# Windowed attention with a gated two-weight product on one core: a 1e-9 moved to ScalarE, three weight conversions moved to VectorE, slots re-ordered

## The chip, the cores and the metric

One NeuronCore of one Trainium2 chip runs the whole program. The metric is the time of one execution in device microseconds (us). Three timed runs of the kernel before gave 752.46 us as their median (751.79 to 753.01); the profiled execution took 752.39 us.

## The reference

```python
scores = q @ k.T / sqrt(64)                      # 4 batches, 8 heads, 768 positions
keep = (pos_k < n_sink) | (0 <= pos_q - pos_k < window)        # 4 sinks, window 128
a = exp(where(keep, scores, -1e9) - rowmax)
a = a / (sum(a) + 1e-9)
x = (a @ v)                                      # to 3072 tokens x 512
out = ((x @ w_a) * (x @ w_b)) @ w_out            # 512 -> 1536 -> 512, float32
```

The weights come as 64-bit words and are turned into float32 on the chip.

## The kernel before

**Tiles and chunks.** Tokens go in tiles of 128. The first tile of each batch is handled by `first_tiles` (L514). The other 20 tiles form six chunks (`CHUNKS`, L229): two of two tiles, four of four tiles. The gated product ("MoE") of a chunk runs while the attention of the next one is computed: stage c=0 (`moe`) works on the first tiles, c=1 and c=2 (`moe2`) on the two small chunks, c=3 to 6 (`moe7`) on the large ones; c=6 has no attention beside it. In the trace c=1 lies at about 145 to 224 us, c=2 to 294, c=3 to 407, c=4 to 525, c=5 to 643.

**Number form.** A float32 operand is split into a high part, rounded to TensorE's fp32r, and a low part, the rest. One product is three matmuls: high by high, high by low, low by high. ScalarE makes high parts by a copy, VectorE or GpSimd (POOL) low parts by a subtraction.

**Slots.** `run` (L1372) and the MoE functions emit the instructions; `keep_order` (L1169) then fixes each engine's order to the order of emission, so an engine never passes over a waiting instruction. A slot is one group of matmuls with what `slot` (L1283) emits behind it: `finish` (the end of the attention scores of the step before: 1e-9 added at L724, reciprocal L725, two scalings by ScalarE L727, a copy L728), the slot's own read of PSUM, `between` (as many attention steps as `PACE` wants), `step_late` (work that was put off, one stage a slot), and `next_piece` (three output matmuls at L1204 for an earlier block of MoE). In `moe2` a round j has three slots: the `a` product read by ScalarE (L990), the `b` product multiplied in by VectorE (L998), and the output products (L983); its g is split at L995 (ScalarE) and L996 (POOL; VectorE in the last round). In `moe7` a half-round has four: X (12 matmuls, read at L1248), Y (12, added at L1252), X again (12, L1258 to L1261), and a short one of 6 into Y (read at L1265). X and Y each have one PSUM bank, and from c=3 on the scores have one bank as well: a score product waits until VectorE has read the one before (L712, L713).

**Seven products.** `moe7` uses seven products in place of eight (the Winograd scheme). The weights' sums for it are made by `convert` (L1011) during c=1 and c=2: fetch two weights from DRAM (L1031), four sums on POOL (L1036, L1037, L1040, L1041), two high parts on ScalarE (L1051), two low parts on VectorE (L1055), each part sent to DRAM by SyncE's queue (L1048). `CONVERTS` says at which slot one begins: c=1 has seven (slots 0, 3, 8, 11, 16, 19, 24), c=2 five. The next chunk's own sums are made by `make_ops` (L1120) in six stages: differences on VectorE (L1141), high parts on ScalarE (L1134), low parts on VectorE (L1138). They begin in c=2 at slot `OPS_AT`, and in c=3 to 5 behind the first product of the last half-round. For c=2 the operand is split by `split_part` (L887, L890 and L891) at slots 34 to 36 of c=1.

**Attention.** Per head, POOL splits keys and queries (L418, L421), TensorE makes scores of a tile (L702), VectorE overwrites part of them and takes the row's limit (L712, L713), ScalarE the exponential with its sum (L715).

## Time and profile before

| | |
|---|---|
| median of three runs | 752.46 us |
| profiled execution | 752.39 us, its span 750.5 us |
| granted TensorE clock | 0.999 of full speed |
| busy: TensorE, its weight loads | 726.9 us (97%), 641.4 us (85%) |
| busy: VectorE, ScalarE, POOL | 475.9 us (63%), 385.0 us (51%), 354.2 us (47%) |

TensorE's row counts a matmul as busy until its modelled end, so idle TensorE time shows as waits, listed by what was waited for. A busy time of another engine includes what an instruction waits for after it was started.

### The profile page before, as it was taken

Reading aid. Unit: us, or ns where it says so; the run is one execution under the profiler, and the core shown is the slowest. Engines: PE = TensorE matmul, PEld = TensorE weight load, DVE = VectorE, ACT = ScalarE, POOL = GpSimd, SP = SyncE. Lnnn points to the kernel's source line nnn. Section 1 sums busy time; section 2 is a strip of 40 time slices with the busy share of each in tenths; the row PEclk is TensorE's granted clock in tenths of the full one; section 3 lists DMA queues with packets and bytes.
Section 4 is the critical chain, followed back from the end, with each engine's and each line's share of the span. In section 5 each row is a group of like instructions: output and inputs, shape, how many; then the busy total and the mean of one; then the engine's idle time right before and its main releaser. Section 6 shows DMA issues by size and latency. Waiting matters only on the chain.

```text
span 750.5 us, 14604 instructions
## 1 busy us (share of the span) xinstructions
PE 726.9 (97%) x4952; PEld 641.4 (85%) x4952; DVE 475.9 (63%) x1309; ACT 385.0 (51%) x1111; POOL 354.2 (47%) x378
## 2 busy tenths in 40 slices
PE   8999999999879999999999999999999999999997
PEld 6877777888769888898888988899899898899995
DVE  6899998365466757756648567755676654744322
ACT  6678775466456665545534554543365552444211
POOL 2200000144966793866733877743776723343430
PEclk9999999999999999999999999999999999999999
DMA  8999962388626587867785596876587666589641
GB/s 329 346 389 336 364 228 92 126 261 264 218 76 203 144 279 239 273 224 242 233 266 197 182 310 233 248 239 220 167 286 241 227 213 209 195 295 338 224 156 60
DMA packets 80642, 175.86 MB, mean 234 GB/s; under 512 B 8624, under 2 KB 26032, under 8 KB 80560
## 3 DMA queue, kind: packets, MB, share of 16 engines
q1 hardware_dynamic: 76960, 168.56, 67.1%
q10 hardware_dynamic: 3600, 6.30, 2.2%
q8 instruction: 41, 0.67, 0.4%
q14 instruction: 41, 0.34, 0.1%
HBM read 144.93 MB, written 29.88 MB: 233 GB/s over the span
## 4 chain that ended last, share of the span: by engine, by line
PE 78%; DMA 6%; POOL 6%; DVE 5%; ACT 3%; issue 1%; SPq 0%; ACTq 0%; POOLq 0%; DVEq 0%
PE o L1204 17%; PE a L906 7%; PE b L906 6%; PE o L933 5%; PE s L702 4%; PE av L745 4%; PE o L983 2%; PE t L733 2%; PE X_0b L1157 2%; PE X_2b L1157 2%; PE X_1b L1157 2%; PE X_2a L1157 2%; PE X_3a L1157 2%; PE X_5a L1157 2%; PE X_4a L1157 2%; PE X_4b L1157 2%
## 5 line engine op out<-in xcount | busy, mean ns | idle before, releaser
L715 ACT ACTIVATE p<-p,st 128x132 f32<-128x132 f32 x128 | 51.7, 404 | 87.7 <-DVE st L713 87.6
L1204 PE MATMUL o<-r_O,gh 128*128 128x512 f32 x288 | 93.8, 407 | 0.0
L1321 POOL TENSOR_TENSOR gl<-bu,gh 128x512 fp32r<-128x512 f32 x46 | 60.4, 1313 | 59.3 <-ACT gh L1318 58.4
L727 ACT ACTIVATE p<-p,st 128x132 f32<-128x132 f32 x128 | 45.0, 399 | 38.3 <-DVE st L725 38.1
L1036 POOL TENSOR_TENSOR s_a<-s_a 128x256 f32<-128x256 f32 x4 | 2.9, 736 | 123.3 <-PE o L933 113.6
L724 DVE TENSOR_SCALAR st<-st 128x2 f32<-128x2 f32 x64 | 33.1, 517 | 42.8 <-ACT p L715 42.8
L712 DVE COPY_PREDICATED s<-own,s 128x128 f32<-128x128 uint16 x128 | 36.9, 288 | 36.8 <-PE s L702 36.5
L1204 PE MATMUL o<-r_O,gl 128*128 128x512 f32 x144 | 56.5, 392 | 0.0
L1253 POOL TENSOR_TENSOR bu<-x 128x256 f32<-128x256 f32 x24 | 18.6, 775 | 72.4 <-DVE x L1252 72.4
L421 POOL TENSOR_TENSOR ks<-kr,ks 64x656 fp32r<-64x656 f32 x32 | 51.3, 1604 | 2.7
L1204 PEld LDWEIGHTS o<-r_O,gh 128*128 128x128 f32 x288 | 44.9, 189 | 2.6 <-issue 2.1
L702 PE MATMUL s<-ks,qh 128*128 128x260 f32 x128 | 39.0, 305 | 3.5 <-DVE st L713 1.9
L421 POOL TENSOR_TENSOR ql<-qr,qh 128x512 fp32r<-128x512 f32 x32 | 41.4, 1292 | 1.3
L906 PE MATMUL a<-x,w_a 128*128 128x256 f32 x288 | 40.2, 287 | 1.5 <-ACT x L890 1.5
L418 POOL TENSOR_SCALAR ks<-kr 64x656 fp32r<-64x656 f32 x32 | 24.5, 764 | 36.5 <-PE s L702 33.6
L735 DVE TENSOR_TENSOR pt<-t,tri 128x1024 f32<-128x1024 f32 x32 | 39.0, 1220 | 4.1 <-PE t L733 4.1
L713 DVE CUSTOM_DVE_ANT_0 p<-s,mg 128x132 f32<-128x132 f32 x128 | 37.8, 295 | 4.4
L906 PE MATMUL b<-x,w_b 128*128 128x256 f32 x288 | 39.3, 285 | 0.0
L906 PEld LDWEIGHTS a<-x,w_a 128*128 128x128 f32 x288 | 36.5, 188 | 2.7 <-ACT x L890 1.7
L1318 ACT CAST gh<-bu 128x512 fp32r<-128x512 f32 x48 | 29.2, 612 | 18.2 <-PE o L1204 11.9
L906 PEld LDWEIGHTS b<-x,w_b 128*128 128x128 f32 x288 | 36.2, 189 | 0.3 <-issue 0.2
L702 PE MATMUL s<-ks,ql 128*128 128x260 f32 x128 | 36.1, 282 | 0.0
(480 smaller groups left out, 2239.4 us busy)
## 6 DMA issues: line engine op xcount, KB each, us to landing
r_O<-d_O SPq DMA_DIRECT2D x36, 512.0 KB, 4.3
r_H_a<-d_H_a SPq DMA_DIRECT2D x24, 512.0 KB, 5.5
r_L_a<-d_L_a SPq DMA_DIRECT2D x24, 512.0 KB, 6.3
r_H_b<-d_H_b SPq DMA_DIRECT2D x24, 512.0 KB, 5.5
r_L_b<-d_L_b SPq DMA_DIRECT2D x24, 512.0 KB, 6.3
qr<-in_qT_dram SPq DMA_DIRECT2D x32, 256.0 KB, 3.8
raw_a<-in_wa_dram SPq DMA_DIRECT2D x12, 512.0 KB, 6.8
raw_b<-in_wb_dram SPq DMA_DIRECT2D x12, 512.0 KB, 6.5
```

The lines of the kernel that those rows point to most:

```text
L421: return self.nc.gpsimd.tensor_tensor(o, i, high.bitcast(F32), op=ALU.subtract)
L702: mm = nc.tensor.matmul(ps, lhsT=q[:, i * P:(i + 1) * P], rhs=ks[:, c0s[i]:c0s[i] + SW], start=n == 0, stop=n == 1)
L712: nc.vector.copy_predicated(ps[:, :P], self.own.bitcast(mybir.dt.uint16), ps[:, W:])
L713: nc.vector.tensor_tensor_reduce(out=p, in0=ps[:, :W], in1=self.mg[:, :W], scale=-0.125, scalar=BIG, op0=ALU.add, op1=ALU.min, accum_out=s ...
L715: nc.scalar.activation(p, p, AF.Exp, bias=st[:, 0:1], scale=-1.0, accum_out=st[:, 1:2])
L727: nc.scalar.mul(p[:, k, :], p[:, k, :], st[:, 3, k:k + 1])
L735: nc.vector.tensor_tensor(self.parted(nt)[:, h % 2].rearrange("p (c m) q -> p c m q", m=2), tp.unsqueeze(2).to_broadcast(shape), self.tri. ...
L906: mm = self.nc.tensor.matmul(ps[:, cols], lhsT=w[:, ksl], rhs=x[:, kk, cols], start=start and kk == 0 and i == 0, stop=kk == NK - 1 and i ...
L933: nc.tensor.matmul(outs[i], lhsT=g[:, sl], rhs=w, start=j == 0 and k == 0, stop=j == NJ - 1 and k == 2)
L1157: mm = self.nc.tensor.matmul(ps, lhsT=a[:, ksl], rhs=b[:, kk, :], start=start and kk == 0 and n == 0, stop=kk == 1 and n == 2, skip_group_ ...
L1204: self.nc.tensor.matmul(outs[t], lhsT=g[:, sl], rhs=w, start=j == 0 and n == 0, stop=j == NJ - 1 and n == 2)
L1321: (V if late else G).tensor_tensor(hl[k][1], halves[k], hl[k][0].bitcast(F32), op=ALU.subtract)
```

## The change

It has six parts. (1) The 1e-9 is added by ScalarE, right behind the exponential of the second tile of a pair, in place of VectorE at L724. (2) In slots with `first=True` the read of PSUM on VectorE is emitted ahead of `finish`, hence ahead of the reciprocal. (3) Conversions that begin in c=1 behind slot 15 (slots 16, 19 and 24) make their four sums on VectorE; in all twelve, the high parts go out by ScalarE's DMA queue, one stage later. (4) The split for c=2 is made in two halves at slots 34 and 35. (5) `make_ops` has seven stages in another order and starts one slot earlier in c=2, and in c=3 to 5 in the short slot ahead of the last half-round. In the last round of `moe2` the split of g is put ahead of other late work. (6) In the short slot (`inside=True`) the attention step and the late work are emitted behind the first of the three output matmuls.

```diff
@@ -48,7 +48,7 @@
...
                 (26, ("w_o3", "w_o4")))}
-OPS_AT = 33
+OPS_AT = 32
 LOAD_AT = 6
@@ -714,6 +714,9 @@
...
             state[h, i] = state["p"], state["st"]
+            if i % 2:
+                st = state["st"]
+                nc.scalar.activation(st[:, 2], st[:, 1], AF.Copy, bias=1e-9)
             if h == 0 and i == 0:
@@ -721,7 +724,6 @@
...
             p, st = state[h, i]
-            nc.vector.tensor_scalar(st[:, 2], st[:, 1], 1e-9, None, op0=ALU.add)
             nc.vector.reciprocal(st[:, 3], st[:, 2])
@@ -889,6 +891,12 @@
...
+
+    def split_half(self, xf, xs, k):
+        k = slice(2 * k, 2 * k + 2)
+        x, (xh, xl) = xf[:, k], xs
+        self.nc.scalar.copy(xh[:, k], x)
+        self.nc.vector.tensor_tensor(xl[:, k], x, xh[:, k].bitcast(F32), op=ALU.subtract)
@@ -968,11 +976,11 @@
...
-        def slot(*moe):
+        def slot(*moe, **how):
             nonlocal count
...
                 self.later(stages)
-            self.slot(between, *moe)
+            self.slot(between, *moe, **how)
             count += 1
@@ -994,8 +1002,11 @@
...
                      [lambda e=e, g=g, gh=gh, gl=gl: e.tensor_tensor(gl, g, gh.bitcast(F32), op=ALU.subtract)]]
-            self.later(parts if j < NJ - 1 else [parts[0] + parts[1]])
-            slot(lambda: V.tensor_tensor(g, pb[:, :n], g, op=ALU.mult))
+            if j < NJ - 1:
+                self.later(parts)
+            else:
+                self.late[:0] = parts[0] + parts[1]
+            slot(lambda: V.tensor_tensor(g, pb[:, :n], g, op=ALU.mult), first=True)
             if prev is not None:
@@ -1008,11 +1019,10 @@
...
-    def convert(self, kind, i, homes):
+    def convert(self, kind, i, homes, g):
...
         tag = f"{kind}{i}"
-        g = nc.gpsimd
         f, h = [], []
@@ -1040,22 +1050,25 @@
...
-        def part(n, x, k):
+        def part(n, x, k, queue=nc.sync):
             key = (n, kind, i)
...
                                               name="d_" + "_".join(map(str, key)))
-            nc.sync.dma_start(self.away[key][:, k * DM:(k + 1) * DM], x.rearrange("p a c -> p (a c)"))
+            queue.dma_start(self.away[key][:, k * DM:(k + 1) * DM], x.rearrange("p a c -> p (a c)"))
...
             nc.scalar.copy(h[k], f[k])
-            part("H", h[k].bitcast(F32), k)
+
+        def send(k):
+            part("H", h[k].bitcast(F32), k, nc.scalar)
...
-        return [[fetch], [], [first], [lambda: high(0), second], [lambda: high(1), lambda: low(0)], [lambda: low(1)]]
+        return [[fetch], [], [first], [lambda: high(0), second],
+                [lambda: high(1), lambda: low(0), lambda: send(0)], [lambda: low(1), lambda: send(1)]]
@@ -1140,11 +1153,12 @@
...
-        return [[high("B11", b11), less(ta, b12, b11, V), less(b12, b22, b12, V)],
-                [low("B11", b11, V), high("T1", ta), less(tb, b22, ta, V)],
-                [low("T1", ta, V), high("T2", tb), high("T3", b12), less(b11, b21, tb, V)],
-                [low("T2", tb, V), low("T3", b12, V), high("B21", b21), high("B22", b22)],
-                [low("B22", b22, V), low("B21", b21, V), high("T4", b11)],
+        return [[less(ta, b12, b11, V), less(b12, b22, b12, V)],
+                [high("B11", b11), high("T1", ta), low("B11", b11, V), less(tb, b22, ta, V)],
+                [high("T2", tb), high("T3", b12), low("T1", ta, V)],
+                [less(b11, b21, tb, V), low("T2", tb, V)],
+                [low("T3", b12, V), high("B21", b21), high("B22", b22)],
+                [low("B21", b21, V), high("T4", b11), low("B22", b22, V)],
                 [low("T4", b11, V)]]
@@ -1188,7 +1202,7 @@
...
-    def project_piece(self, c, i, rows, outs, gs, k, last):
+    def project_piece(self, c, i, rows, outs, gs, k, last, inside):
@@ -1202,6 +1216,8 @@
...
             self.nc.tensor.matmul(outs[t], lhsT=g[:, sl], rhs=w, start=j == 0 and n == 0, stop=j == NJ - 1 and n == 2)
+            if inside and n == 0:
+                inside()
         if t == NT - 1 and j < KEPT:
@@ -1221,8 +1237,8 @@
...
-        def slot(*moe):
-            self.slot(between, *moe)
+        def slot(*moe, **how):
+            self.slot(between, *moe, **how)
@@ -1235,7 +1251,7 @@
...
                 w = lambda name: self.operand(c, kind, i, name)
-                ready = following and end and ki == 1
+                ready = following and end and ki == 0
                 first, v12, v21, v22 = (quarter(bv if ki else av, k) for k in range(4))
@@ -1243,26 +1259,26 @@
...
                 self.product(X1, w("S1"), ops["T1"], False, lead)
-                if ready:
-                    self.later(lambda: self.make_ops(following(), self.tmp))
                 slot(lambda: A.copy(x, X), lambda: ahead(2 * i + ki, 0))
...
                 self.product(Y[:, HN:], w("S3"), ops["T3"], False, lead)
-                slot(lambda: V.tensor_tensor(x, Y, x, op=ALU.add))
+                slot(lambda: V.tensor_tensor(x, Y, x, op=ALU.add), first=True)
                 self.late.append(lambda v22=v22, u2=u2, w2=w2: G.tensor_tensor(v22, u2, w2, op=ALU.add))
...
                 if ki == 0:
-                    slot(lambda: V.tensor_copy(first, X0), lambda: V.tensor_tensor(v12, X1, u2, op=ALU.add))
+                    slot(lambda: V.tensor_copy(first, X0), lambda: V.tensor_tensor(v12, X1, u2, op=ALU.add), first=True)
                 else:
                     slot(lambda: V.tensor_tensor(first, X0, quarter(av, 0), op=ALU.mult),
-                         lambda: V.tensor_tensor(v12, X1, u2, op=ALU.add))
+                         lambda: V.tensor_tensor(v12, X1, u2, op=ALU.add), first=True)
                     self.late.append(lambda v12=v12: G.tensor_tensor(v12, v12, quarter(av, 1), op=ALU.mult))
...
                 self.product(Y[:, HN:], w("A22"), ops["T4"], False)
-                slot(lambda: V.tensor_tensor(v21, Y[:, HN:], u2, op=ALU.add))
+                if ready:
+                    self.later(lambda: self.make_ops(following(), self.tmp))
+                slot(lambda: V.tensor_tensor(v21, Y[:, HN:], u2, op=ALU.add), first=True, inside=True)
                 if ki == 1:
@@ -1280,13 +1296,21 @@
...
-    def slot(self, between, *moe):
-        self.finish()
+    def slot(self, between, *moe, first=False, inside=False):
+        if not first:
+            self.finish()
         for f in moe:
             f()
-        between()
-        self.step_late()
-        self.next_piece()
+        self.finish()
+
+        def attend():
+            between()
+            self.step_late()
+
+        if not inside:
+            attend()
+        if not self.next_piece(attend if inside else None) and inside:
+            attend()
@@ -1326,20 +1350,21 @@
...
-    def next_piece(self):
+    def next_piece(self, inside=None):
         if not self.queue:
-            return
+            return False
         c, i, rows, outs, gs, k, last = self.queue[0]
         if len(gs) <= k // NT:
-            return
+            return False
         self.queue.pop(0)
-        self.project_piece(c, i, rows, outs, gs, k, last)
+        self.project_piece(c, i, rows, outs, gs, k, last, inside)
+        return True
...
             xf = self.cp.tile([P, NK, 2 * P], F32, tag="xfA", name=f"xf{tag}")
-            return [xf[:, kk, :] for kk in range(NK)], None
+            return [xf[:, kk, :] for kk in range(NK)], xf
         xf = [self.cp.tile([P, 2, NT * P], F32, tag=t, name=f"{t}{tag}") for t in ("xfA", "xfB")]
@@ -1449,12 +1474,12 @@
...
                     if at == s:
-                        yield self.convert("ab"[n % 2], n // 2, homes)
+                        yield self.convert("ab"[n % 2], n // 2, homes, self.nc.vector if c == 1 and s > 15 else self.nc.gpsimd)
                 if c == 1:
...
                         yield [[lambda: send_o(j)]]
-                    for kk in {34: (0,), 35: (1, 2), 36: (3,)}.get(s, ()):
-                        yield [[lambda kk=kk: self.split_part(made[1][0], xs2, kk)]]
+                    if s in (34, 35):
+                        yield [[lambda k=s - 34: self.split_half(made[1][1], xs2, k)]]
                     return
...
                     yield [[lambda: self.shift(j // 2)], [lambda: self.fetch(min(4, j // 2 + 1))]]
```

## Rows read from the trace of the kernel before

**Rows 1.** The page's part 1: busy us, share of the span, instructions of each engine.

```profile
PE 726.9 (97%) x4952; PEld 641.4 (85%) x4952; DVE 475.9 (63%) x1309; ACT 385.0 (51%) x1111; POOL 354.2 (47%) x378
```

**Rows 2.** Waits of TensorE, whole span: us in total, times, longest us.

```profile
PE o L983 <- POOL gl L996: 2.5, 3, 1.5
PE s L702 <- DVE st L713: 1.9, 4, 0.9
PE a L906 <- ACT x L890: 1.5, 1, 1.5
PE Y_0a L1157 <- DVE opw_o L1138: 1.3, 3, 0.4
PE o L983 <- ACT gh L995: 1.3, 1, 1.3
...
PE X_0a L1157 <- DVE opw_o L1138: 1.0, 3, 0.6
...
PE s L702 <- POOL ql L421: 1.3, 1, 1.3
...
PE t L733 <- ACT p L727: 0.9, 1, 0.9
...
PE s L814 <- DMA kx<-in_kD_dram: 0.6, 1, 0.6
PE o L1204 <- POOL gl L1321: 0.6, 2, 0.3
PE X_0a L1157 <- ACT x L1248: 0.4, 1, 0.4
PE s L702 <- POOL ks L418: 0.3, 1, 0.3
...
PE o L983 <- DVE gl L996: 0.3, 1, 0.3
```

**Rows 3.** Lines L724 and L725: duration ns min/median/max, first and last start, forms.

```profile
L724 DVE TENSOR_SCALAR st<-st x64: 165/386/1372, 201.3 to 615.0; 128x2 f32<-128x2 f32 x64
...
L725 DVE RECIPROCAL st<-st x64: 165/166/168, 201.6 to 615.2; 128x2 f32<-128x2 f32 x64
```

**Rows 4.** Timeline, 215.9 to 219.6 us: start, us, instruction, idle before.

```profile
215.94 1.59 POOL L421 TENSOR_TENSOR ks<-kr,ks 64x656 fp32r<-64x656 f32 x1
...
216.19 1.37 DVE L724 TENSOR_SCALAR st<-st 128x2 f32<-128x2 f32 x1 [0.57 <-ACT p L715]
...
217.68 0.40 DVE L998 TENSOR_TENSOR g<-b,g 128x256 f32<-128x256 f32 x1
...
219.09 0.39 ACT L995 CAST gh<-g 128x256 fp32r<-128x256 f32 x1
```

**Rows 5.** Busy time in 184 to 214 us (PE, PEld, DVE, ACT, POOL), clock, DMA.

```profile
184.00:214.00 30.00, 26.25 (x187) 22.75 (x187) 14.22 (x49) 13.82 (x43) 27.55 (x29) 1.00 0.58 203
```

**Rows 6.** Timeline, 192.4 to 197.9 us.

```profile
192.42 0.73 POOL L1036 TENSOR_TENSOR sf_b<-sf_b 128x256 f32<-128x256 f32 x1
...
194.63 1.26 POOL L421 TENSOR_TENSOR ql<-qr,qh 128x512 fp32r<-128x512 f32 x1
...
196.62 0.69 DVE L1055 TENSOR_TENSOR sf_b<-sf_b,sh_b 128x512 fp32r<-128x512 f32 x1 [5.33 <-POOL sf_b L1040]
196.67 1.24 POOL L1041 TENSOR_TENSOR sf_b<-sf_b 128x256 f32<-128x256 f32 x1
```

**Rows 7.** Lines L891 and L1063: duration ns min/median/max.

```profile
L891 DVE TENSOR_TENSOR x<-xf,x x8: 415/418/426, 139.6 to 224.5; 128x256 fp32r<-128x256 f32 x8
...
L1063 ACTq DMA_DIRECT2D d_F_a<-wf_a x12: 326/327/348, 21.6 to 119.1; - x12
```

**Rows 8.** Groups by line, ScalarE, 144 to 745 us: busy, mean ns, idle before.

```profile
L728 ACT COPY sc<-p 128x8 f32<-128x8 f32 x64 | 12.7, 198 | 2.0
```

**Rows 9.** Timeline, 408.2 to 410.5 us.

```profile
408.28 1.60 POOL L1324 TENSOR_TENSOR bu<-bu,av 128x512 f32<-128x512 f32 x1 [1.03 <-DVE bu L1265]
...
408.66 1.77 DVE L1138 TENSOR_TENSOR opw_o<-xfA,opw_o 128x512 fp32r<-128x512 f32 x1
```
## The prediction

> **What bounds the kernel now.** I read the page's busy times first. TensorE is busy 726.9 us of a span of 750.5 us [rows 1], so at most 23.6 us are to be had without fewer matmuls, and the change leaves every matmul in place. The list of TensorE's waits comes next. The thirteen entries that lie behind 145 us add up to 13.9 us [rows 2]; the other idle time is the start (inputs, the first weights) and the end (last copy, last store), which no part touches. So the question is which of these 13.9 us go, and which new waits come. Each of the thirteen is short and has a late instruction on another engine ahead of it, so I followed each back in the timeline. What to see there: an engine that is half idle on average is late because of what stands ahead of one instruction in its queue.
>
> Two patterns carry most of it. First, L724 adds 1e-9 to 128x2 numbers. Alone it takes 0.165 us, but its median is 0.386 and its longest 1.372 us, while the reciprocal on the same numbers takes 0.165 to 0.168 us in all 64 cases [rows 3]. The longest began at 216.19 while POOL's L421 ran from 215.94 for 1.59 us, and ended within 0.04 us of it [rows 4]: L724 waits for POOL's instruction to end. Behind it in VectorE's order stand L998 (at 217.68) and thus ScalarE's L995 (219.09), for which TensorE waited 1.3 us [rows 2, 4]. Second, from 184 to 214 us POOL is busy 27.55 of 30 us, VectorE 14.22 and TensorE only 26.25 [rows 5]. There POOL does three conversions beside the splits of keys, queries and g, and TensorE waits for ql and gl [rows 2].
>
> **The change, part by part.** The sum is made against the profiled execution, 752.4 us (span 750.5 and 1.9 around it); the median, 752.46, is the same.
>
> (1) The 1e-9 on ScalarE. 64 instructions leave VectorE and with them its holds by POOL. On ScalarE there is no row of this operation; the nearest is L728, a small copy of 0.198 us [rows 8], so 64 x 0.198 = 12.7 us go to an engine that is busy 51% [rows 1]. The chain from exponential to reciprocal is then 0.03 us longer than with an unheld L724 (0.198 against 0.165) and up to 1.17 us shorter than with a held one. The waits for "st L713" (four, 1.9 us) are for VectorE reading the scores' only bank behind a held L724; I let 1.6 of them go and keep 0.3. Of the 1.3 us for gh, L998 comes some 1.2 us earlier, but ScalarE's next exponential still stands ahead of L995, and its scalings need the reciprocal; I take 0.5. Gain 2.1; bounds 0 and 3.2 (both waits whole).
>
> (2) PSUM reads ahead of the reciprocal. VectorE waited for the exponential with the sum of PSUM behind it; now it waits for the matmuls. No TensorE wait of its own hangs on it; I count it inside (1). Cover: from the score to the transposes that need the scaled row there are two slots. If that cover is gone the 0.9 us of "t L733 waits for p L727" grows: at most doubled, -0.9. I take 0, and I also leave that 0.9 where it is, since ScalarE was behind POOL's L1041 there, in c=2, where POOL keeps the sums.
>
> (3) Three conversions' sums on VectorE. 12 sums of 0.73 us leave POOL [rows 6], 8.8 us or more out of its 27.55, and its queue stops being the last: ql's 1.3 and gl's 2.5 us hang on it. I take 3.4 of 3.8; 0.4 stays for a gl that finds POOL in a long L421. VectorE gets 12 x 0.418 = 5.0 us (L891, the same form) [rows 7], on top of 14.22 of 30. In this order they stand ahead of score reads and L998, and each can be held by POOL: L1055 and L1041, both with two inputs in SBUF, exclude each other (L1041 began 0.05 us behind L1055 and took 1.24 in place of 0.73 us) [rows 6]. Bounds for the hold: nothing, and 1.59 us each [rows 4], 19.1 in all. VectorE has 30 - 14.2 - 5.0 = 10.8 us of cover. Holds overlap it mostly; I take 1.3 us on the path, near the low end, because L1055, which stood under the same condition, cost 0.69 in the row where it ran against POOL. The Trainium skill, "SBUF — State Buffer", section "Who interferes with whom", says that a VectorE instruction with two SBUF inputs contends with a POOL instruction that reads SBUF, and that whoever issues first holds the port for the whole instruction. That speaks against these sums on VectorE; by it alone, with the longest POOL instruction met each time, the charge would be the upper bound above.
>
> The sums also wait for their fetch, which POOL met far ahead of its slot; VectorE comes to them only in the slot, two slots behind the fetch, when I expect the data to be there. The fetch of the third is issued behind other SyncE work, so some of the 1.3 is for that.
>
> High parts on ScalarE's queue: 24 issues of 0.327 us [rows 7] leave SyncE, which held key loads behind them (0.6 us for kx). I take 0.2 of it. On ScalarE an issue stands one stage behind the copy it sends, so it waits for nothing; it costs its 0.327 us only where ScalarE is late: 24 x 0.327 = 7.8 us as the upper bound, 0 as the lower. With 12.7 us of (1) I charge 0.4 together.
>
> (4) Split in two halves at slots 34 and 35: the last quarter at slot 36 was what "a waits for x L890" (1.5 us) ended on. A half is there one slot sooner; 1.3 of 1.5 goes. Bounds 0 and 1.5.
>
> (5) Sums of the next chunk. Three times Y_0a (1.3 us) and X_0a (1.0) wait for low parts L1138, and two gl's (0.6) stand behind them. At 408.66 the low part of T3 was held by POOL's L1324, 1.77 us [rows 9]. In the new order T2's low part is made a slot earlier and T3's stands directly behind the read of Y, ahead of L1324, so the first wait goes. But L1138 of B11 now shares a slot with the copy that it needs, and with a difference behind it, some 0.7 us each (L1055 has their size) [rows 6]; VectorE's L1252 stands behind both, and Y's short product needs L1252. Of 2.9 I let 1.7 go; bounds 2.9, and -0.9 if L1252 is late by 0.3 us at three boundaries. In c=2 the same start one slot earlier, and g's split ahead of it, take 0.4 of 0.7 (X_0a for x L1248, o for VectorE's gl).
>
> (6) Scores inside the output products move by one output matmul; they come later behind a gap that was short and leave the next a little shorter. No row prices it: between +0.3 (what (1) leaves) and -1.9 (the "st L713" waits back); I take 0. The 0.3 us for ks, a key load, stays.
>
> Sum: 2.1 + 3.4 + 0.2 + 1.3 + 1.7 + 0.4 = 9.1 us gained, less 1.3 + 0.4 = 1.7: 7.4. **752.4 - 7.4 = 745.0 us.**
>
> **The rivals.**
> (A) The boundaries gain nothing: (5) only moves the wait to Y's short product behind L1252. For it speaks the 1.4 us now ahead of L1252, against it that T3 gets clear of L1324. It takes away 2.1 and adds 0.2 at three places: 747.7 us.
> (B) Nearly all of the 13.9 us go, because each wait's cause is removed and VectorE has cover: some 2.5 stay (t, ks, part of gh and kx), 11.4 gained: 741.0 us. Against it: order on ScalarE.
> (C) ScalarE becomes the late engine: the issues and additions stand ahead of exponentials, gh and x. If all 7.8 us of issues were on the path instead of my 0.4: 745.0 + 7.4 = 752.4, no change. Against it: 51% busy, and no issue waits.
> (D) Slower: VectorE is held in 184 to 214 us, by POOL or for a fetch, in the twelve moved sums, and score reads and L998 queue behind. It eats the cover of 10.8 us first. My gain without the 1.3 is 8.7, so it decides from 10.8 + 8.7 = 19.5 us of holds, 1.63 us a sum, a little over POOL's usual 1.59. At 1.77 each, the longest hold seen [rows 9], it is 21.2: 752.4 - 8.7 + 21.2 - 10.8 = 754.1 us. Against it: POOL has 8.8 us less to do just there. The rule of the Trainium skill, "SBUF — State Buffer", "Who interferes with whom", is what would bring these holds about.
> (E) The change doesn't do what it says: the reciprocal takes over L724's hold. Then 2.1 falls away: 747.1 us. Against it: never over 0.168 us in 64 [rows 3].
>
> **How the numbers follow.** Forecast (743 to 747) 0.51; A 0.19, E 0.04, B 0.10, C 0.08, D 0.08. A measurement of this kernel can tell about 0.2% (1.5 us) from no change, so faster (under 750.9) is the forecast, A, B and E: 0.84; same is C, 0.08; slower is D, 0.08. The range reaches from B's time to between A and C, 741.0 to 751.0, and leaves out D, most of C and the far half of B, some 0.19.
>
> **What would show it.** L724 gone, the reciprocal 0.17 us, "st L713" near nothing (1); ql and gl of L983 under 0.5 us in all and POOL idle between 184 and 214 us (3); VectorE's sums there 0.42 us each, and under 1 us where held, against D; x L890 under 0.3 (4); Y_0a and X_0a under 0.4 us a boundary, and no new wait of Y_5b for L1252 (5, A); span about 743. It is wrong if TensorE's listed waits behind 145 us add up to over 10 us, or if its busy time rises.

## The result, and the profile after

Against the kernel before on the same chip, the changed kernel took 735.23 us (median of 4 runs, 734.77 to 737.31) where before took 752.74 (4 runs): a ratio of 0.9771, 95% interval 0.9745 to 0.9796. Run again later on another occasion it took 736.28 us against 753.37, ratio 0.9783 (0.9764 to 0.9801). The sign was forecast; the size was not: 17.5 us in place of 7.4, and the time lies under the range's low end of 741.0.

Part 1 of the page of the changed kernel, against [rows 1]:

```profile
PE 721.1 (98%) x4952; PEld 641.8 (87%) x4952; DVE 451.8 (61%) x1255; ACT 396.1 (54%) x1173; POOL 346.0 (47%) x366
```

There are as many matmuls as before, and their weight loads take as long (641.8 against 641.4 us), but TensorE's busy time has fallen by 5.8 us. That is the first sign of what went wrong in the forecast, which took busy time for a floor.

TensorE's waits behind 150 us in the changed kernel, all of them (us in total, times, longest), against [rows 2]:

```profile
PE t L735 <- ACT p L729: 0.9, 1, 0.9
PE o L1218 <- POOL gl L1345: 0.8, 1, 0.8
PE o L991 <- ACT gh L1003: 0.7, 2, 0.4
PE o L991 <- DVE gl L1004: 0.5, 1, 0.5
PE av L850 <- DVE ptx L840: 0.5, 1, 0.5
PE s L702 <- DVE st L713: 0.4, 1, 0.4
PE a L914 <- DVE x L899: 0.3, 1, 0.3
```

Lines have moved on by up to 24 (L1004 was L996). Of the names, gh and gl are the high and low part of g, t the transposes of the scaled rows, ptx VectorE's copy of transposes, av the product with the values, and kx keys that a DMA loads. Every listed wait of Y_0a, X_0a, ql and kx is gone; 13.9 us of listed waits have become 4.1. But the time fell by more than the list lost. Busy time in the stretch from the start of c=1's first product to that of the last product, first the kernel before (start:end, length, then busy us and instructions of PE, PEld, DVE, ACT, POOL, then clock, DMA share, GB/s), and under it the border to c=4 and c=4 without its two borders:

```profile
147.41:744.68 597.27, 583.39 (x4152) 525.75 (x4151) 355.46 (x1020) 286.83 (x891) 344.67 (x353) 1.00 0.68 224
404.58:421.66 17.08, 16.17 (x108) 14.28 (x107) 12.46 (x28) 7.75 (x20) 11.16 (x11) 1.00 0.53 175
421.66:518.25 96.59, 96.59 (x700) 87.48 (x699) 60.45 (x186) 47.15 (x158) 61.33 (x62) 1.00 0.75 248
```

The same three stretches of the changed kernel, and the 30 us that answer to [rows 5]:

```profile
150.11:729.73 579.62, 575.47 (x4152) 524.31 (x4151) 331.44 (x966) 297.88 (x953) 336.54 (x341) 1.00 0.68 231
398.27:413.62 15.35, 15.35 (x109) 14.29 (x108) 11.59 (x26) 6.70 (x19) 11.85 (x11) 1.00 0.59 194
413.62:508.63 95.01, 95.01 (x701) 86.91 (x699) 52.73 (x171) 50.62 (x176) 61.40 (x62) 1.00 0.75 251
186.70:216.70 30.00, 29.09 (x210) 26.50 (x209) 25.10 (x65) 17.61 (x57) 22.63 (x21) 1.00 0.52 178
```

The stretch is 17.65 us shorter. Of the 30 us TensorE is busy 29.09 (before 26.25) and POOL 22.63 (before 27.55). Idle TensorE time in the whole stretch went from 13.88 (597.27 - 583.39) to 4.15 us, a gain of 9.73; the other 7.92 us came out of busy time. c=4 shows it pure: no idle time in either kernel, and 1.58 us gained. (The changed kernel's profiled execution, 737.31 us, began c=1 at 150.11 for a wait of 2.8 us at 32 us; another execution of it, without that wait, began c=1 at 146.58. So the stretch from c=1 on is what is compared below.)

**Where busy time hides lateness.** Timeline of the kernel before (start, us, instruction), first in c=4, then at the border to c=4:

```profile
433.66 1.59 POOL L421 TENSOR_TENSOR ks<-kr,ks 64x656 fp32r<-64x656 f32 x1
434.33 0.94 DVE L724 TENSOR_SCALAR st<-st 128x2 f32<-128x2 f32 x1 [0.56 <-ACT p L715]
435.31 0.17 DVE L725 RECIPROCAL st<-st 128x2 f32<-128x2 f32 x1
435.39 0.42 DVE L1265 TENSOR_TENSOR av<-Y_1a,x 128x256 f32<-128x256 f32 x1
435.73 0.28 DVE L712 COPY_PREDICATED s<-own,s 128x128 f32<-128x128 uint16 x1
436.05 0.30 DVE L713 CUSTOM_DVE_ANT_0 p<-s,mg 128x132 f32<-128x132 f32 x1
436.24 0.28 PE L1157 MATMUL X_1b<-opw_o,r_L_b 128*128 128x256 f32 x1
436.27 0.08 DVE L713 DVE_READ_ACCUMULATOR2_ANT st<- 128x1 f32 x1
436.50 0.36 PE L702 MATMUL s<-ks,qh 128*128 128x260 f32 x1
436.70 0.28 PE L702 MATMUL s<-ks,ql 128*128 128x260 f32 x1
...
409.66 0.28 PE L1157 MATMUL Y_0a<-opw_o,r_L_a 128*128 128x256 f32 x1
409.78 0.28 PE L1157 MATMUL Y_0a<-opw_o,r_H_a 128*128 128x256 f32 x1
410.49 0.39 PE L1157 MATMUL Y_0a<-opw_o,r_H_a 128*128 128x256 f32 x1 [0.43 <-DVE opw_o L1138]
```

A matmul over 256 columns is busy for 0.28 us, but the next one is due 0.12 us after its start (409.66, 409.78). A start that comes 0.26 us after the one before it (436.24, 436.50) has lost 0.14 us, and the list shows no idle time; the second score product loses 0.08 more (0.20 apart). At 410.49 the list says 0.43, and the loss is 0.71 - 0.12 = 0.59. So about 0.16 us of each late start, and the whole of a shorter one, is booked as busy. What was late at 436.50 is the chain of [rows 4] once more: L724 held by L421 (0.94 us), the reciprocal, the read of Y, the score's reads L712 and L713, done at 436.35, then the weight load and the product. In c=4 of before I count in the trace's starts 18 such places around L702, 1.50 us in all; the changed kernel has none there, and that is all but 0.08 of its 1.58 us. The same count over the whole stretch from c=1 on, each start against the usual distance for its pair of shapes, finds 7.7 to 7.9 us less of such hidden lateness in the changed kernel: some 5.4 at score products, 1.7 at X and Y behind the borders, 0.9 at output products.

The page's rows of these products say it too. Groups of L702 in the kernel before (busy us, mean ns, then idle time before):

```profile
L702 PE MATMUL s<-ks,qh 128*128 128x260 f32 x128 | 39.0, 305 | 3.5 <-DVE st L713 1.9 <-POOL ql L421 1.3 <-POOL ks L418 0.3
```

and in the changed kernel:

```profile
L702 PE MATMUL s<-ks,qh 128*128 128x260 f32 x128 | 36.4, 285 | 0.4 <-DVE st L713 0.4
```

One form, one count, and 20 ns less on the mean: 2.6 us that were waits. The Trainium skill, "Trainium Kernel Development and Optimization", section "Performance Expectations", calls matmul busy time a bad metric for how close a kernel is to its limit, because matmuls are pipelined, and the busy share of weight loads a good one; that agrees with these rows, in which the weight loads stayed within 0.4 us.

### The profile page after: what moved, and what is told of

Read it like the earlier page. It is cut to its first block, busy times and chain, and to the rows that moved or that the text cites. A ratio compares the mean times of both kernels' runs of the same rounds, so it can differ in the third digit from the quotient of the medians.

```text
span 735.6 us, 14612 instructions
## 1 busy us (share of the span) xinstructions
PE 721.1 (98%) x4952; PEld 641.8 (87%) x4952; DVE 451.8 (61%) x1255; ACT 396.1 (54%) x1173; POOL 346.0 (47%) x366
## 4 chain that ended last, share of the span: by engine, by line
PE 85%; DMA 5%; POOL 4%; DVE 3%; ACT 1%; issue 1%; SPq 0%; ACTq 0%; POOLq 0%; DVEq 0%
PE o L1218 18%; PE a L914 8%; PE b L914 8%; PE o L941 5%; PE av L747 4%; PE s L702 3%; PE o L991 3%; PE s L816 2%; PE t L735 2%; PE X_2b L1171 2%; PE X_5b L1171 2%; PE X_3b L1171 2%; PE X_1b L1171 2%; PE X_4a L1171 2%; PE X_2a L1171 2%; PE X_3a L1171 2%
## 5 line engine op out<-in xcount | busy, mean ns | idle before, releaser
L1218 PE MATMUL o<-r_O,gh 128*128 128x512 f32 x288 | 97.7, 407 | 0.0
L712 DVE COPY_PREDICATED s<-own,s 128x128 f32<-128x128 uint16 x128 | 36.7, 287 | 52.6 <-PE s L702 52.0
L729 ACT ACTIVATE p<-p,st 128x132 f32<-128x132 f32 x128 | 44.9, 398 | 31.3 <-DVE st L727 31.2
L1046 POOL TENSOR_TENSOR s_a<-s_a 128x256 f32<-128x256 f32 x2 | 1.5, 732 | 119.4 <-PE o L941 115.7
L421 POOL TENSOR_TENSOR ks<-kr,ks 64x656 fp32r<-64x656 f32 x32 | 51.7, 1615 | 2.7
L1218 PEld LDWEIGHTS o<-r_O,gh 128*128 128x128 f32 x288 | 46.5, 189 | 2.6 <-issue 2.1
L421 POOL TENSOR_TENSOR ql<-qr,qh 128x512 fp32r<-128x512 f32 x32 | 41.5, 1296 | 1.3
L713 DVE CUSTOM_DVE_ANT_0 p<-s,mg 128x132 f32<-128x132 f32 x128 | 37.8, 295 | 4.4
L702 PE MATMUL s<-ks,qh 128*128 128x260 f32 x128 | 36.4, 285 | 0.4 <-DVE st L713 0.4
L702 PE MATMUL s<-ks,ql 128*128 128x260 f32 x128 | 36.2, 283 | 0.0
L1348 POOL TENSOR_TENSOR bu<-bu,av 128x512 f32<-128x512 f32 x23 | 30.6, 1331 | 8.7 <-DVE bu L1281 8.2
```

The costliest lines, as they stand in the source:

```text
L421: return self.nc.gpsimd.tensor_tensor(o, i, high.bitcast(F32), op=ALU.subtract)
L702: mm = nc.tensor.matmul(ps, lhsT=q[:, i * P:(i + 1) * P], rhs=ks[:, c0s[i]:c0s[i] + SW], start=n == 0, stop=n == 1)
L712: nc.vector.copy_predicated(ps[:, :P], self.own.bitcast(mybir.dt.uint16), ps[:, W:])
L713: nc.vector.tensor_tensor_reduce(out=p, in0=ps[:, :W], in1=self.mg[:, :W], scale=-0.125, scalar=BIG, op0=ALU.add, op1=ALU.min, accum_out=s ...
L729: nc.scalar.mul(p[:, k, :], p[:, k, :], st[:, 3, k:k + 1])
L1218: self.nc.tensor.matmul(outs[t], lhsT=g[:, sl], rhs=w, start=j == 0 and n == 0, stop=j == NJ - 1 and n == 2)
```

## The experiments

Lengths of stages are worked out from starts of matmuls in each kernel's profiled execution: the products into a, b, o, X and Y, 3,768 in every kernel, are counted in order, and each column runs from one fixed product to another. "To c=4" is the border from the last half-round of c=3 to the second half-round of c=4, and so on; c=6 (90.3 us, no attention beside it) never changes, so the products themselves take as long in every kernel. Each length comes from one execution. For the first two rows the length in us, for the others the difference to the kernel named (a point is under 0.1).

| kernel | c=1 | c=2 | to c=3 | c=3 | to c=4 | c=4 | to c=5 | c=5 | to c=6 | c=1 to end |
|---|---|---|---|---|---|---|---|---|---|---|
| before | 74.30 | 72.83 | 8.94 | 101.10 | 17.08 | 96.59 | 19.59 | 103.21 | 13.29 | 597.27 |
| changed | 69.17 | 71.47 | 8.54 | 98.98 | 15.34 | 95.01 | 17.85 | 101.27 | 11.68 | 579.62 |
| *to before:* e2 | -0.25 | +1.44 | -0.60 | -1.86 | . | -0.77 | . | -1.11 | . | -3.21 |
| e10 | +0.16 | . | -0.18 | -1.32 | . | -1.40 | . | -1.71 | . | -4.43 |
| e11 | -2.85 | -1.58 | -0.60 | +0.16 | . | . | . | -0.32 | . | -5.21 |
| *to changed:* again | . | . | . | -0.78 | . | . | . | . | . | -0.68 |
| e1 | +0.97 | . | . | +1.41 | . | +0.18 | . | +0.19 | . | +2.67 |
| e5 | +0.91 | . | . | +0.88 | . | +0.86 | . | +0.78 | . | +3.44 |
| e6 | +1.43 | . | . | . | . | . | . | . | . | +1.44 |
| e3 | +3.56 | . | . | -0.44 | . | . | . | . | . | +3.11 |
| e7 | +3.47 | . | . | . | . | . | . | . | . | +3.49 |
| e8 | +0.21 | +1.47 | . | . | . | . | . | . | . | +1.65 |
| e4 | +0.76 | -0.60 | +1.30 | +0.63 | +1.74 | +0.23 | +1.76 | . | +1.60 | +7.38 |
| e12 | +0.93 | +1.26 | . | +0.11 | . | . | . | . | . | +2.25 |
| e9 | . | +1.13 | . | -0.49 | . | . | . | . | . | +0.57 |
| e13 | +0.55 | +0.47 | . | +0.13 | . | +0.29 | . | . | . | +1.39 |
| e14 | +0.74 | +0.46 | . | -0.48 | . | +0.23 | . | . | . | +0.91 |

Two executions of the same kernel differ in c=3 by 0.78: the gl of its first block (0.8 in the list above) is late in some executions and not in others. In c=1 a wait for a key load (kx, 0.4 to 1.2 us) comes and goes likewise. Differences of that size in these two columns are not laid to an edit.

### The scores' reads: parts (1), (6) and (2)

**e1**: the changed kernel with part (1) undone.

```diff
-                nc.scalar.activation(st[:, 2], st[:, 1], AF.Copy, bias=1e-9)
...
+            nc.vector.tensor_scalar(st[:, 2], st[:, 1], 1e-9, None, op0=ALU.add)
```

> The changed kernel with the 1e-9 back on VectorE (one instruction per pair of tiles, in front of the reciprocal), all else as changed. Theory H (hold): VectorE's addition is held by POOL's key split, score products come late, and each late product costs TensorE about 0.15 us more than the idle time that the list shows. Then the time rises by 4 to 6 us over the changed kernel (to 739 to 741), 1.2 to 2 us in each of the three large stages that have attention beside them, though the list of waits grows by 2 us at most. Theory O (order): the small waits at scores went because PSUM reads and scores were re-ordered; then it rises by 0 to 2 us.

737.85 us, ratio to before 0.9796 (0.9766 to 0.9827); 2.67 us lost from c=1 on (0.45 of it at a late key in c=1), but only 0.18 and 0.19 in c=4 and c=5. So the addition alone is not where the large stages got their 1.6 and 1.9 us.

**e2**: the kernel before with part (1) alone.

```diff
+                nc.scalar.activation(st[:, 2], st[:, 1], AF.Copy, bias=1e-9)
...
-            nc.vector.tensor_scalar(st[:, 2], st[:, 1], 1e-9, None, op0=ALU.add)
```

> The kernel before with only the 1e-9 moved to ScalarE. Theory H: 4 to 6 us faster than before (747 to 749), with the waits for the limits of L713 gone from the list and the short gaps at score products gone too. Theory O: 0 to 2 us faster (751 to 753).

748.87 us, 0.994 (0.992 to 0.9961). Here it does bring 0.77 us in c=4, where no wait is listed, and 1.11 in c=5, where one of 0.4 is (st L713), and nothing at the borders after c=3. The 3.2 us from c=1 on lie between the ranges of the two theories, as do the 2.7 of e1. In c=2 it lost 1.44 us: VectorE's gl was 0.8 us later than before (1.1 us listed in two, against 0.3).

**e5**: the changed kernel with part (6) undone: in the short slot the attention step is emitted ahead of the output products again.

```diff
-    ..., first=True, inside=True)
+    ..., first=True)
```

> The changed kernel with the short slot's attention step ahead of all three output matmuls again. If this move is worth nothing, as the prediction has it, the time stays within 0.5 us of the changed kernel and the large stages keep their lengths. Rival: it is what keeps the scores' one bank free, since a score product follows the one before after 18 matmuls in place of 6; then 1 us is lost in each of the three large stages, 2.5 to 3.5 us in all.

738.23 us, 0.9804 (0.9785 to 0.9823). It lost 0.88, 0.86 and 0.78 us in the three large stages, with no new entry in the list of waits there.

**e10**: the kernel before with parts (2) and (6) alone.

```diff
...
-                slot(lambda: V.tensor_tensor(v21, Y[:, HN:], u2, op=ALU.add))
+                slot(lambda: V.tensor_tensor(v21, Y[:, HN:], u2, op=ALU.add), first=True, inside=True)
...
```

> The kernel before with only the re-ordering inside a slot: PSUM read ahead of the reciprocal, and the short slot's attention step behind the first of three output matmuls; the addition stays on VectorE, the conversions, the split and the next chunk's sums stay as they were. Theory L (either the held addition goes or the score product gets later; each alone frees most of the late score products): 1.3 to 2 us shorter in each of the three large stages, as with the whole change, nothing at the boundaries, 4 to 6 us in all (747 to 749). Rival: order and addition are worth only what they lose when undone, 0.8 us a stage; then 2.5 to 3.5 us.

747.47 us, 0.9923 (0.9903 to 0.9942): 1.32, 1.40 and 1.71 us gained in the large stages, the 1e-9 still on VectorE. So a score product is saved from waiting for L713 in two ways, an earlier L713 (e2) or a later product (e10). c=4 got 0.77 by one, 1.40 by the other and 1.58 by all together: either undone alone (e1, e5) loses less than it can bring alone.

**e6**: the changed kernel with part (2) undone, the reciprocal ahead of the slot's read everywhere.

```diff
-        if not first:
-            self.finish()
+        self.finish()
```

> The changed kernel with the reciprocal back ahead of the slot's read of PSUM on VectorE, in every slot. If reading PSUM first is worth nothing now that the addition is on ScalarE: within 0.5 us of the changed kernel. Rival: VectorE waits for ScalarE's sum with PSUM unread behind it; then 0.3 to 1 us lost in each large stage and up to 1 us in the first small chunk's stage.

736.4 us, 0.9783 (0.9763 to 0.9803). The large stages don't move; c=1 is 1.43 us longer. Waits of TensorE in this kernel:

```profile
PE av L850 <- DVE ptx L840: 1.0, 1, 1.0
...
PE s L816 <- DMA kx<-in_kD_dram: 0.4, 1, 0.4
```

There is 0.5 us more for ptx, VectorE's copy behind the reciprocal, and two products of late keys, which by their starts lost 0.87 us. With these taken off the part is worth about 0.6 us, and only in c=1. That rests on one execution: the medians can't tell this kernel from the changed one (735.23 and 736.28 us).

### The 30 us in which POOL was the last: part (3)

**e3**: the changed kernel with the three conversions' sums back on POOL.

```diff
-  ... self.convert(..., self.nc.vector if c == 1 and s > 15 else self.nc.gpsimd)
+  ... self.convert(..., self.nc.gpsimd)
```

> The changed kernel with the sums of the last three conversions of the first small chunk's stage back on POOL. Theory P (POOL was the late engine from 184 to 214 us): 3 to 5 us slower than the changed kernel, all of it in that stage, with ql and gl back among TensorE's waits. Rival: the queue changes did it (high parts on ScalarE's queue, reads first); then under 1 us slower.

738.67 us, 0.981 (0.9779 to 0.984); c=1 is 3.56 us longer, and the two waits of [rows 2] are back, gl as long as it was:

```profile
PE o L991 <- POOL gl L1004: 2.5, 3, 1.6
...
PE s L702 <- POOL ql L421: 0.4, 1, 0.4
```

The move has a price too: TensorE's wait for ptx (0.5 us in the changed kernel) is listed neither here nor in the kernel before, and at that place e3 is 0.90 us ahead. The copy to ptx stands behind two of the moved sums, the held L1046 among them.

**e7**: the changed kernel with the high parts on SyncE's queue.

```diff
-            part("H", h[k].bitcast(F32), k, nc.scalar)
+            part("H", h[k].bitcast(F32), k)
```

> The changed kernel with the conversions' high parts sent by SyncE's queue, still one stage later. Theory: the queue is worth 0.2 to 0.6 us (the wait for keys, which the changed kernel no longer has), all of it in the first small chunk's stage. Rival: ScalarE's 24 issues cost something and the time falls by up to 1 us.

738.66 us, 0.9817 (0.9789 to 0.9844); c=1 is 3.47 us longer. Waits of TensorE in this kernel:

```profile
PE s L702 <- DVE st L713: 1.3, 2, 0.9
PE s L816 <- DMA kx<-in_kD_dram: 1.2, 1, 1.2
...
PE av L850 <- DVE ptx L840: 0.9, 1, 0.9
```

Who waited for the fetches of L1041 in the same kernel (us, times):

```profile
  DVE s_a L1047: 1.8, 2
```

In the changed kernel no VectorE sum waits for a fetch. So on SyncE's queue the fetches fall behind the sends, and VectorE, which now makes the sums, waits 1.8 us for them with the score's reads queued behind. The fetch that it waits longest for (1.61 us) is issued 0.43 us behind the send of a high part, 51.2 us into c=1; in the changed kernel it is issued 48.3 us into it, and TensorE is only 1.8 us behind the changed kernel there. So the first edit of part (3) loses most of its worth without the second; a kernel with both undone was not run. The late keys lost 1.33 us by their start; with that taken off, 2.1 us remain.

**e11**: the kernel before with parts (3) and (4) alone.

```diff
-                        yield self.convert("ab"[n % 2], n // 2, homes)
+                        yield self.convert("ab"[n % 2], n // 2, homes, self.nc.vector if c == 1 and s > 15 else self.nc.gpsimd)
...
-                        yield [[lambda kk=kk: self.split_part(made[1][0], xs2, kk)]]
+                        yield [[lambda k=s - 34: self.split_half(made[1][1], xs2, k)]]
...
```

> The kernel before with only the conversions' sums and queue and the split in halves. If the first small chunk's stage is all theirs: 4 to 5 us shorter there and nothing elsewhere (748 to 749). If the held addition on VectorE spoils it, since VectorE now has twelve more instructions that POOL can hold: 1 to 3 us (750 to 752).

747.36 us, 0.9927 (0.99 to 0.9954): c=1 gains 2.85 of the 5.13 us that all parts bring there, c=2 1.58. What is left in c=1 is listed: st L713 2.0, gh 1.7, kx 1.1 and ptx 1.0 us.

**What the moved sums met.** Timeline of the changed kernel:

```profile
191.54 1.96 POOL L421 TENSOR_TENSOR ks<-kr,ks 64x656 fp32r<-64x656 f32 x1
191.96 1.82 DVE L1046 TENSOR_TENSOR sf_b<-sf_b 128x256 f32<-128x256 f32 x1
```

L1046, 0.42 us elsewhere, began behind POOL's L421 and lasted past its end. The rule of the Trainium skill, "SBUF — State Buffer", "Who interferes with whom", is seen at work here. But the twelve sums took 8.6 us in all, by their durations in the trace, 3.5 over twelve times 0.418 [rows 7]; rival D needed 19.5 us of holds.

### The split: part (4)

**e8**: the changed kernel with the split in quarters at slots 34 to 36.

```diff
-                    if s in (34, 35):
-                        yield [[lambda k=s - 34: self.split_half(made[1][1], xs2, k)]]
+                    for kk in {34: (0,), 35: (1, 2), 36: (3,)}.get(s, ()):
+                        yield [[lambda kk=kk: self.split_part(made[1][0], xs2, kk)]]
```

> The changed kernel with the operand of the second small chunk split in one, two and one quarters at slots 34 to 36 again. Theory: 1.2 to 1.7 us lost, at the border of the two small chunks' stages, with the wait of a for x back in the list. Rival: the split was late only because VectorE was held; then under 0.4 us.

738.09 us, 0.9809 (0.9789 to 0.9829); c=2 is 1.47 us longer and its wait is back:

```profile
PE a L914 <- ACT x L892: 1.2, 1, 1.2
```

### The next chunk's sums: part (5)

**e4**: the changed kernel with the six old stages of `make_ops`, started where before started them. The earlier split of g in the last round of `moe2` stays.

```diff
-OPS_AT = 32
+OPS_AT = 33
...
-                ready = following and end and ki == 0
+                ready = following and end and ki == 1
```

> The changed kernel with the next chunk's sums in the six old stages and at their old start. Theory B (the held low part of T3 cost 1.6 to 1.75 us at each of three boundaries, twice what the list shows): 4.5 to 5.5 us slower than the changed kernel, at the boundaries alone. Rival: part of it comes from the other edits, and only the listed 0.9 us a boundary returns: 2 to 3 us slower.

742.26 us, 0.9847 (0.9816 to 0.9879). The borders lose 1.74, 1.76 and 1.60 us, what the change had gained there, and the border to c=3 1.30; c=2 gains 0.60. With c=3 and c=4 it comes to 6.7 us, of which up to 0.8 in c=3 may be the gl that varies. Waits of TensorE in this kernel:

```profile
PE Y_0a L1170 <- DVE opw_o L1151: 1.5, 4, 0.4
PE X_0a L1170 <- DVE opw_o L1151: 1.0, 3, 0.6
...
PE X_0a L1170 <- ACT x L1263: 0.8, 1, 0.8
```

The changed kernel at the border to c=4, timeline, against [rows 9]:

```profile
401.57 0.68 DVE L1151 TENSOR_TENSOR opw_o<-xfA,opw_o 128x512 fp32r<-128x512 f32 x1
401.79 1.62 POOL L1348 TENSOR_TENSOR bu<-bu,av 128x512 f32<-128x512 f32 x1 [1.03 <-DVE bu L1281]
402.82 1.13 DVE L1151 TENSOR_TENSOR opw_o<-xfB,opw_o 128x512 fp32r<-128x512 f32 x1
```

T3's low part now begins ahead of POOL's product and takes 0.68 us in place of 1.77; it is POOL's product that comes second, and nothing waits for it there. The next low part takes 1.13, and Y_0a doesn't wait for it.

### Two attempts to go further

**e12**: the changed kernel with one more conversion's sums (slot 18 of c=2) on VectorE. **e9**: as e12, and c=3's first block has its product and low parts on VectorE.

```diff
-  self.nc.vector if c == 1 and s > 15 else self.nc.gpsimd
+  self.nc.vector if (c, s) == (2, 18) or c == 1 and s > 15 else self.nc.gpsimd
...
-                    self.turn(c, i, gs, last and end)
+                    self.turn(c, i, gs, last and end or (c, i) == (3, 0))
```

> The changed kernel with the sums of one more conversion, at slot 18 of the second small chunk's stage, on VectorE. The wait of t for p (0.9 us listed, 1.2 with the restart) stands behind ScalarE's high part, which waits for POOL's L1041: if so it goes and the time falls by 0.8 to 1.3 us, in that stage alone. Rival: VectorE is the late one there (49 of 71 us busy before); then no change or up to 1 us slower.

> The same, and in the first large stage the first block's product and low parts on VectorE in place of POOL, against the wait of o for POOL's gl (0.8 us listed). If both causes are read rightly, 1.6 to 2.3 us faster than the changed kernel; if VectorE's added instructions only move the wait to the scores' bank, 0 to 1.3 us.

737.4 us, 0.9785 (0.9763 to 0.9807) and 736.83 us, 0.9784 (0.9764 to 0.9804): neither better than the changed kernel. In e12 the wait for the scaled row grew from 0.9:

```profile
PE t L735 <- ACT p L729: 2.4, 1, 2.4
```

Two of the moved sums were held, one behind POOL's L1004 (0.82 us) and one behind its L421 (1.39 us), and the exponential and its scaling came later. The same edit that paid in c=1 costs 1.26 us in c=2; that VectorE's instructions behind it are nearer to being the last there is how I read it, and no run tests it.

**The changed kernel again, e13 and e14**, on one chip: in e13 ScalarE's copy L1082, which stands ahead of the scaling L729, comes a stage later; e14 has c=3's first split on VectorE too (the second line of e9's edit).

```diff
-                    yield [[lambda: self.shift(j // 2)], [lambda: self.fetch(min(4, j // 2 + 1))]]
+                    yield [[], [lambda: self.shift(j // 2)], [lambda: self.fetch(min(4, j // 2 + 1))]]
```

> The changed kernel once more, to stand beside the two below on one chip. If the 17.5 us of the first measurement are the kernel's and not that chip's, the ratio to the kernel before is within 0.2% of 0.977. Its c=2 takes some 71.5 us, its c=3 inside some 99 us.

> The changed kernel with the copy of a weight half on ScalarE (L1082) one stage later. Theory S (the 0.9 us that remain of the wait for the scaled row stem from the order on ScalarE, where this copy stands ahead of the scaling): the wait falls under 0.4 us and c=2 is 0.4 to 0.8 us shorter than in the changed kernel beside it. Theory V (it stems from VectorE, held by POOL ahead of the row's limit, and the copy filled time that ScalarE waited anyway): wait and c=2 as before within 0.2 us.

> As the run with the copy later, and c=3's first block splits its g on VectorE in place of POOL. If listed waits tell less than is lost, the listed 0.8 us for gl fall by about 0.4 and c=3 by 0.5 or more against the run with the copy later; if they tell all of it, by 0.4 or less. No other stage changes by over 0.2 us.

736.28 us, 736.19 (0.9779, 0.9755 to 0.9802) and 737.99 (0.9793, 0.9766 to 0.9819): no gain. Waits of TensorE in e13:

```profile
PE o L1218 <- POOL gl L1345: 1.1, 1, 1.1
PE o L991 <- POOL gl L1004: 0.9, 1, 0.9
...
PE t L735 <- ACT p L729: 0.3, 1, 0.3
```

Theory S was right on the wait, which fell from 0.9 (0.8 in the repeat) to 0.3, so ScalarE's order set it, and wrong on the time: c=2 is 0.47 us longer (0.44 against the repeat). A new wait for gl stands 2.9 us further on. Timeline of e13 there:

```profile
268.45 1.03 DVE L1067 TENSOR_TENSOR sf_b<-sf_b,sh_b 128x512 fp32r<-128x512 f32 x1
268.89 1.18 POOL L1004 TENSOR_TENSOR gl<-g,gh 128x256 fp32r<-128x256 f32 x1
```

L1004, mostly 0.74 us, came behind VectorE's L1067 and took 1.18; in the changed kernel beside it L1004 came first and L1067 took 1.20 in its place. In e14 the listed gl of c=3 is 0.4 against e13's 1.1, and c=3 0.61 us shorter: no more than the list says. That is not against the hidden 0.16 us: a wait that is shortened and still there keeps its hidden part; only one that goes altogether gives it back. The changed kernel run again shows it at the same place: its entry for gl (0.8) is gone, but the product still starts 0.40 us after the one before it, where 0.23 is usual, and c=3 is shorter by 0.78 us, no more than the list lost.

## Why the prediction was wrong in size, and right in sign

**The step that failed** is the first: "at most 23.6 us are to be had without fewer matmuls", and after it "which of these 13.9 us go". Both take a listed wait for all that is lost; that idle TensorE time shows as waits, as the profile's section says, holds here only for what exceeds some 0.16 us a start. Where waits went altogether, more came back: a border's 0.91 us of idle time was 1.74 us of lost time, c=4 lost 1.58 us with none listed, and from c=1 on 9.73 us of idle time were 17.65 us. Of the 10.25 us by which those exceed the forecast 7.4, 7.92 were lateness booked as busy; the other 2.33 are idle time, of which more went, net of new waits, than forecast. My test for being wrong (listed waits over 10 us, or a busy time that rises) could not show this error, as both went the other way.

By parts, each measured by undoing it; they overlap, so they add to more than 17.65:

- (1) Forecast 2.1, measured 2.2 to 2.7 in the changed kernel (without and with the late key) and 3.2 alone. The waits for st L713 went as forecast, to 0.4. The bound of 3.2, "both waits whole", was no bound, since most late score products in c=3 to c=5, all 18 places of c=4 among them, had no entry.
- (2) Forecast 0, measured about 0.6 (1.43 with late keys), all in c=1, by the copy to ptx, which I had not followed. The 0.9 us for t that I left where it was, "since ScalarE was behind POOL's L1041", hung on ScalarE's copy L1082 as well (e13).
- (3) Sums: forecast 3.4 - 1.3, measured 3.6. The hold was real, 3.5 us on twelve sums, but most of it was covered: with them on VectorE c=1 is shorter by 3.6 us, and the price of 1.3 shows as 0.9 at ptx. Queue: forecast 0.2 less a share of 0.4, measured 2.1 to 3.5. I had looked for who was late behind SyncE in before, where POOL met its fetches early; with the sums on VectorE the fetch has a customer that can't wait. That sentence stood in the prediction ("two slots behind the fetch, when I expect the data to be there"), but the queue that makes it true was charged elsewhere.
- (4) Forecast 1.3, measured 1.5: right.
- (5) Forecast 1.7 + 0.4, measured 6 to 6.7: the largest miss. At the three borders it brought 5.1 us in place of 1.7; before's idle time there was 2.9 (17.08 us with TensorE busy 16.17, 19.59 with 18.68, 13.30 with 12.22), all of it went, and with it the hidden parts. In c=2 with the border to c=3 it brought 0.7 (1.30 - 0.60) in place of 0.4, the rest lies in c=3 and c=4. The earlier split of g was not undone; its wait, o for VectorE's gl, did not fall (0.3 before, 0.5 after). Rival A's mechanism, Y's short product behind L1252, is not in the list.
- (6) Forecast 0, measured 0.8 to 0.9 us in each large stage. "No row prices it" was true of the list, not of the trace: the distances between starts around L702 would have.

Of the rivals, B came nearest in time: the listed waits fell by 9.8 of its 11.4 us, and it too stopped at the list. C fell: with 24 issues and 64 additions more on ScalarE no listed wait for it grew from c=1 on (t 0.9 as before, gh 0.7 from 1.3). D fell by the size of the holds, though two of the twelve sums (1.82 and 1.39 us) were held longer than the 1 us that I had set as the sign of it; e12 shows its mechanism where cover is short. E fell: the reciprocal stayed at 0.151 to 0.166 us in all 64 cases.

What stays open: why the key load of c=1 and the gl of c=3 are late in some executions; no run set them. How much of the borders' gain is the new order of `make_ops` and how much its earlier start was not run apart, nor what the later stage of the sends is worth, which e7 keeps.

## What to carry to other kernels

Price a late matmul by the distance of its start from the one before it, against the distance of neighbours in the same stream; the list of waits leaves out 0.16 us of each here, and everything where instructions are late by less. Undo parts one at a time and also make them alone: two edits that each cure the same lateness look small when undone and don't add. Before moving work to another engine, follow its fetches too: an engine that met its data early hides a late queue, and the new one may not.

## What the runs showed of the hardware that was not expected

- An instruction of 128x2 numbers on VectorE took up to 1.37 us behind POOL [rows 3], while the reciprocal on the same numbers never did. The Trainium skill, "SBUF — State Buffer", "Who interferes with whom", names tensor_scalar among the operations that can take the port pair shared with POOL, which fits L724. On ScalarE the addition took 0.203 to 0.207 us in all 64 cases.
- Who is first decides: at 401.57 VectorE's low part kept its 0.68 us ahead of POOL's product, at 408.66 in the kernel before it took 1.77 behind it [rows 9]. The gain at the borders comes with another order and an earlier start of the same operations, not with less work.
